# Issuing the 512-column products of one batch's MLP as two products of 256 columns

## The chip, the cores and the metric

The kernel runs on one core of a Trainium2 chip. The metric is the device time of one execution in microseconds (us), the median of several runs. TensorE multiplies, VectorE (DVE in the rows), ScalarE (ACT) and GpSimd (POOL) do the elementwise work, and the SP queue issues most transfers.

## What is computed

For every batch b (8 of them) and head h (8), the reference lets 512 tokens of width 64 read from 32 state vectors and the state vectors read from the tokens. The heads are then joined and everything goes through one MLP with a squared ReLU:

```python
scores = scale * np.matmul(x, state.transpose(0, 1, 3, 2))      # softmax over the states
xread = np.matmul(a, state)
scores2 = scale * np.matmul(state, x.transpose(0, 1, 3, 2))     # softmax over the tokens
sread = np.matmul(a2, x)
attn = np.concatenate([xread, sread], axis=2)                   # (8, 8, 544, 64)
x = attn.transpose(0, 2, 1, 3).reshape(8 * 544, 512)
h = np.maximum(x @ w_in, 0.0)                                   # w_in: 512 x 2048
return (h * h @ w_out).astype(np.float32)                       # w_out: 2048 x 512
```

## The kernel before

**Tiles and stages.** The MLP rows are worked through in nine blocks: one of 512 tokens for each batch (blocks 0 to 7), and a last one of 256 rows that holds the state reads of all batches (block 8). In blocks 0 to 7 the first layer is not applied to the token reads. Instead the state vectors are multiplied into `w_in` beforehand (tiles `w2`), so that the first layer of a block is a product of the softmax weights (tiles `k_hi`, `k_lo`) with `w2`. The hidden width of 2048 is cut into 16 chunks `fc` of 128.

**Three products for one.** To keep the precision, each operand is a pair of fp32r tiles, a high part and a low part. The helper `mm3` (its `T.matmul` is line 346) issues, for each pair of operands, high by high, high by low and low by high, all into the same PSUM tile. Every product has its own weight load.

**One chunk of a batch.** `hidden(blk, fc)` makes `ph`, a PSUM bank of 128 hidden features by 512 tokens: two contractions of 128 by three products, six products of 512 columns. ScalarE and VectorE then make the squared ReLU and split it into `g_hi` and `g_lo` (lines 898 to 906). `accumulate` takes each of the four 128-token tiles of `g` as the stationary operand and multiplies it with the chunk of `w_out` (512 columns, `wo`), again through `mm3`, into one of four PSUM accumulators `acc`: twelve products of 512 columns. So a chunk has 18 products of 512 columns, and the four accumulators of a batch are filled over all 16 chunks.

**The last block.** `hidden_reads(fc)` (lines 916 and 917) alternates products of 512 columns, where high and low parts lie side by side, with products of 256 columns, four of each in a chunk. Its second layer has two token tiles, so six products of 512 columns.

**Order.** The order of all steps is written out by hand (the strings `FIRST`, `BLOCK`, `LAST`, `READS`) and kept on each engine by `keep_order`. In batch 7 (`LAST`), `hidden.7.(n+1)` is followed by `accumulate.7.n`, with a few steps of the attention of block 8 between them. The last `accumulate.7.15` comes after `hidden.8.0`, so it lies in `READS`.

Of the kernel before, what the change touches and what calls it, by code (L numbers as in the profile page):

```python
# [239 lines left out]
def tile_attn_moe(  # L240
# [17 lines left out]
    B, H, S, D = x.shape  # L258
    Ns = state.shape[2]
    DM, DFF = w_in.shape  # L260
    P = 128
    G = 2
# [14 lines left out]
    KC = S // P  # L277
    V, A, T, SP, PL = nc.vector, nc.scalar, nc.tensor, nc.sync, nc.gpsimd
    traced, last = [0], {}
# [39 lines left out]
    def plain_w2(b, hb):  # L319
        return f"plain_w2.{b}.{hb}" in second  # L320
# [3 lines left out]
    def plain_wo(b, fc):  # L324
        return f"plain_wo.{b}.{fc}" in second
# [9 lines left out]
    def evac(key, out, src):  # L335
        if key in second:
            V.tensor_copy(out, src)  # L337
        else:
            A.copy(out, src)  # L339

    def mm3(ps, pairs, first=True, last=True):
        seq = []
        for (lh, ll), (rh, rl) in pairs:
            seq += [(lh, rh), (lh, rl), (ll, rh)]
        for i, (l, r) in enumerate(seq):
            T.matmul(ps, l, r, start=first and i == 0, stop=last and i == len(seq) - 1)  # L346
# [3 lines left out]
    def keep_busy(key, ps):  # L350

        for _ in range(BUSY.get(key, 0)):
            T.matmul(ps, ones, ones, start=True, stop=True)
# [484 lines left out]
    wo, wo_raw, wo_f = {}, {}, {}  # L838
# [30 lines left out]
    def hidden(blk, fc):  # L869
        cs = ts(fc % 2, P)  # L870
        ph = ps_h.tile([P, S], F32, tag="ph", name=f"ph{blk}_{fc}")
        keep_busy(f"hidden.{blk}.{fc}", ph[:, :P])
        if plain_w2(blk, fc // 2):
            w, k = weights[blk, fc // 2], kf[blk]
            for c in range(G):
                if c and fc < 2:
                    yield
                assert key("token_softmax", blk, c) in done
                T.matmul(ph, w[c][:, cs], k[:, c], start=c == 0, stop=c == G - 1)  # L879
        else:  # L880
            khi, klo = ks[blk]
            whi, wlo = weights[blk, fc // 2]
            mm3(ph, [((whi[:, c, cs], wlo[:, c, cs]), (khi[:, c], klo[:, c])) for c in range(khi.shape[1])])
        yield
        if plain_wo(blk, fc):
            g = p2.tile([P, S], F32, tag="g_hi", name=f"gf{blk}_{fc}", bufs=GB)
            if f"square.{blk}.{fc}" in second:
                A.activation(ph, ph, AF.Relu)
                A.activation(g, ph, AF.Square)
            else:  # L890
                r = p2.tile([P, S], F32, tag="g", name=f"r{blk}_{fc}", bufs=2)
                A.activation(r, ph, AF.Relu)
                V.scalar_tensor_tensor(g, ph, 0.0, r, ALU.max, ALU.mult)
            return g, None
        ghi = p2.tile([P, S], F32R, tag="g_hi", name=f"g_hi{blk}_{fc}", bufs=GB)
        glo = p2.tile([P, S], F32R, tag="g_lo", name=f"g_lo{blk}_{fc}", bufs=LB)
        if f"square.{blk}.{fc}" in second:
            A.activation(ph, ph, AF.Relu)  # L898
            A.activation(ph, ph, AF.Square)  # L899
        else:  # L900
            r = p2.tile([P, S], F32, tag="g", name=f"r{blk}_{fc}", bufs=2)
            A.activation(r, ph, AF.Relu)  # L902
            V.scalar_tensor_tensor(ph, ph, 0.0, r, ALU.max, ALU.mult)  # L903
        evac(f"ghi.{blk}.{fc}", ghi, ph)
        yield
        V.tensor_sub(glo, ph, ghi.bitcast(F32))  # L906
        return ghi, glo
# [19 lines left out]
        V.tensor_sub(glo, r, ghi.bitcast(F32))  # L927
        return ghi, glo

    def accumulate(acc, fc, g, tiles, first, last):  # L930
        ghi, glo = g
        for i in tiles:
            if glo is None:
                T.matmul(acc[i], ghi[:, ts(i, P)], wo[fc], start=first, stop=last)
                continue
            mm3(
                acc[i],
                [((ghi[:, ts(i, P)], glo[:, ts(i, P)]), (wo[fc][:, 0], wo[fc][:, 1]))],
                first=first,
                last=last,  # L940
            )

    out_v = out.rearrange("(b s) f -> b s f", b=B)

# [10 lines left out]
    def store(blk, acc, add):  # L955
        for i in range(KC):
            o = p2.tile([P, DM], F32, tag="o", name=f"o{blk}_{i}", bufs=OB) if add is None else add[i]
            if add is None:
                evac(f"out.{blk}.{i}", o, acc[i])
            else:  # L960
                V.tensor_add(o, acc[i], o)  # L961
            if blk < NX:
                SP.dma_start(out_v[blk, :S].rearrange("(p k) f -> k p f", k=KC)[ORDER[i]], o)
            else:
                SP.dma_start(out_v[blk, ts(i, P)], o)

    def keep_part(blk, acc):
        for i in range(KC):
            o = p2.tile([P, DM], F32, tag="o", name=f"po{blk}_{i}", bufs=OB)
            evac(f"part.{blk}.{i}", o, acc[i])  # L970
            SP.dma_start(part_d[blk][i], o)
# [10 lines left out]
    ks, weights, att, accs, gs = {}, {}, {}, {}, {}  # L982
# [8 lines left out]
    def step_hidden(blk, fc):  # L991
        if blk < B:
            ks[blk] = att[blk].k
            gs[blk, fc] = yield from hidden(blk, fc)
        else:
            gs[blk, fc] = yield from hidden_reads(fc)

    def step_reads(fc, i):
        if fc == 0 and i == 0:
            accs[B] = [ps_acc.tile([P, DM], F32, tag="acc", name=f"acc{B}_{t}") for t in range(B * Ns // P)]  # L1000
        accumulate(accs[B], fc, gs[B, fc], [i], fc == 0, fc == NFC - 1)
        yield
        if fc == NFC - 1:
            store_reads(i, accs[B][i])
# [3 lines left out]
    def step_accumulate(blk, fc):  # L1008
        sums = blk, blk < NS and fc >= PART[blk]
        of = NFC if blk >= NS else NFC - PART[blk] if sums[1] else PART[blk]  # L1010
        count[sums] = count.get(sums, 0) + 1
        first, last = count[sums] == 1, count[sums] == of
        if first:
            accs[blk] = [ps_acc.tile([P, DM], F32, tag="acc", name=f"acc{blk}_{fc}_{t}") for t in range(KC)]
        accumulate(accs[blk], fc, gs.pop((blk, fc)), range(KC), first, last)
        yield
        if last and blk < NS and not sums[1]:
            keep_part(blk, accs.pop(blk))
        elif last:
            store(blk, accs.pop(blk), parts.pop(blk, None))  # L1020

    def key(name, *index):
        return ".".join([name, *map(str, index)])
# [21 lines left out]
    for n in range(B + LATE):  # L1045
# [10 lines left out]
        if n == 0:  # L1056
            for g in range(G):
                tiles = [key("prep", n, j) for j in range(2 * g, 2 * g + 2)]
# [39 lines left out]
    for m in range(HF):  # L1098
        both = whole(f"o{m}")
        for i in range(2):  # L1100
            fc = 2 * m + i
# [16 lines left out]
    for blk in range(B + 1):  # L1118
# [14 lines left out]
        for fc in range(NFC):  # L1133
            hb = fc // 2
            if blk == B:
                needs = ["move_sread", key("split_wi", hb)]
            else:
                w = max(h for h in sets(blk) if h <= hb)
                if blk < NS and fc >= PART[blk]:
                    needs = [key("split_k", blk, g) for g in range(G)]  # L1140
                elif blk:
                    needs = [key("softmax", blk, *g) for g in groups(blk)]
                else:
                    needs = [key("token_softmax", blk, g) for g in range(1 if fc < 2 else G)]
                    needs += [key("split_kf", blk, g) for g in range(G) if hb in NP]
                needs.append(key("w2", blk, w))
            step(key("hidden", blk, fc), step_hidden, blk, fc, after=needs)
            needs = [key("hidden", blk, fc), prepared[fc] if plain_wo(blk, fc) else key("split_wo", fc // 2)]
            needs += [key("load_part", blk)] * (blk < 2 and fc == NFC - 1)
            if blk < B:  # L1150
                step(key("accumulate", blk, fc), step_accumulate, blk, fc, after=needs)
                continue
            for i in range(B * Ns // P):
                step(key("accumulate", blk, fc, i), step_reads, fc, i, after=needs)
# [50 lines left out]
```

## Time and profile before

| what | value |
|---|---|
| time before, median of 3 runs | 648.98 us (648.92 to 649.53) |
| span of the profiled execution | 647.3 us, from the first to the last instruction |
| its own time beside the span | not listed separately; the median of the runs lies 1.7 us above the span |
| TensorE products | 3738, busy 99% of the span |
| mean granted TensorE clock | 1.000 |

The span leaves out what lies before the first and behind the last instruction. A product's duration in the rows runs from its start to its last result, so neighbouring products overlap. The time that a product takes from the next one is the distance of their starts.

### The profile page before, as it was taken

To read this page: it belongs to the slowest core of one execution; us is meant where nothing else is said; L and a number is where in the kernel's file an instruction comes from. 1 tells how busy PE (TensorE), PEld (TensorE's weight loads), DVE (VectorE), ACT (ScalarE), POOL (GpSimd) and SP (SyncE) were. 2 spreads that over 40 slices of the span, in tenths; PEclk is the share of its full clock that TensorE was granted. 3 is DMA by queue.
4 is the path that set the end of the run, shared out by engine and by line. 5 is a ranking of instruction groups with operands and counts; after the bars stand their busy time and mean duration, and the time that the engine had idled before them with its cause. 6 is when DMAs were issued, how large, how long until landed. Compare 5 with 4: busy or idle time off the path is not lost.

```text
span 647.3 us, 9689 instructions
## 1 busy us (share of the span) xinstructions
PE 638.0 (99%) x3738; PEld 503.0 (78%) x3738; DVE 402.8 (62%) x660; ACT 368.8 (57%) x625; POOL 8.6 (1%) x16
## 2 busy tenths in 40 slices
PE   7999999999999999999999999999999999999997
PEld 6677777777777777777787888788878887888885
DVE  5999766665676788766855635564547444325664
ACT  6987658854756755756554535454446443544542
POOL 1200000000000000000000000000000000000000
PEclk9999999999999999999999999999999999999999
DMA  8983947250521866251254702481237321610101
GB/s 319 369 200 101 276 104 198 71 131 10 160 63 58 235 164 199 46 134 66 95 181 113 153 32 99 102 145 51 99 69 144 86 96 33 168 38 2 65 1 33
DMA packets 136590, 76.19 MB, mean 118 GB/s; under 512 B 103264, under 2 KB 121440, under 8 KB 136544
## 3 DMA queue, kind: packets, MB, share of 16 engines
q1 hardware_dynamic: 135584, 75.05, 42.5%
q8 instruction: 29, 0.48, 0.3%
q10 hardware_dynamic: 960, 0.52, 0.3%
q14 instruction: 17, 0.14, 0.1%
HBM read 50.38 MB, written 25.17 MB: 117 GB/s over the span
## 4 chain that ended last, share of the span: by engine, by line
PE 92%; DVE 3%; ACT 2%; DMA 1%; issue 0%; SPq 0%
PE acc L346 55%; PE ph L346 26%; PE w2ps L358 2%; PE ph L916 2%; PE qps L793 2%; PE ph L917 1%; PE pr L673 1%; PE sc L358 1%; DMA xn<-in_x_dram 1%; PE ph L879 1%; DMA out_dram<-o 1%; DVE o L961 0%; PE tsc L358 0%; ACT s L769 0%; PE px L472 0%
## 5 line engine op out<-in xcount | busy, mean ns | idle before, releaser
L346 PE MATMUL acc<-wo,g_hi 128*128 128x512 f32 x1088 | 336.7, 391 | 0.0
L346 PEld LDWEIGHTS acc<-wo,g_hi 128*128 128x128 f32 x1088 | 202.7, 188 | 46.4 <-issue 3.3
L346 PE MATMUL acc<-wo,g_lo 128*128 128x512 f32 x544 | 212.0, 390 | 0.4 <-DVE g_lo L906 0.4
L346 PE MATMUL ph<-k_hi,w 128*128 128x512 f32 x504 | 176.3, 394 | 0.0
L906 DVE TENSOR_TENSOR g_lo<-ph,g_hi 128x512 fp32r<-128x512 f32 x128 | 88.0, 688 | 112.4 <-ACT g_hi L339 111.6
L346 PEld LDWEIGHTS acc<-wo,g_lo 128*128 128x128 f32 x544 | 102.1, 188 | 23.2 <-DVE g_lo L906 1.0
L346 PEld LDWEIGHTS ph<-k_hi,w 128*128 128x128 f32 x504 | 94.6, 188 | 29.5 <-issue 8.0
L898 ACT ACTIVATE ph<-ph 128x512 f32<-128x512 f32 x99 | 57.8, 584 | 87.5 <-PE ph L346 86.0
L346 PE MATMUL ph<-k_lo,w 128*128 128x512 f32 x252 | 98.2, 390 | 0.0
L339 ACT CAST g_hi<-ph 128x512 fp32r<-128x512 f32 x117 | 68.7, 587 | 26.8 <-DVE ph L903 21.2
L899 ACT ACTIVATE ph<-ph 128x512 f32<-128x512 f32 x99 | 57.6, 582 | 3.1
L346 PEld LDWEIGHTS ph<-k_lo,w 128*128 128x128 f32 x252 | 47.3, 188 | 9.3
L903 DVE SCALAR_TENSOR_TENSOR ph<-ph,r 128x512 f32<-128x512 f32 x29 | 20.2, 698 | 48.9 <-ACT r L902 48.9
L902 ACT ACTIVATE r<-ph 128x512 f32<-128x512 f32 x29 | 17.3, 598 | 43.0 <-PE ph L346 43.0
L785 ACT CAST q<-wi 64x512 fp32r<-64x512 f32 x32 | 19.8, 619 | 15.0 <-PE qps L793 12.6
L797 DVE COPY qo<-qps 128x512 f32<-128x512 f32 x32 | 20.6, 683 | 9.7 <-PE qps L793 7.1
L754 DVE TENSOR_TENSOR w<-w2ps,w 128x512 fp32r<-128x512 f32 (+1 forms) x34 | 20.1, 634 | 8.0 <-ACT w L339 8.0
L339 ACT CAST w<-w2ps 128x512 fp32r<-128x512 f32 (+1 forms) x26 | 13.6, 567 | 20.2 <-DVE w L337 11.5
L788 DVE TENSOR_TENSOR q<-wi,q 64x512 fp32r<-64x512 f32 x32 | 22.0, 686 | 1.9 <-ACT q L785 1.0
L916 PE MATMUL ph<-sr,s 128*128 128x512 f32 x64 | 23.1, 396 | 0.0
L358 PE MATMUL w2ps<-wi,stT 64*32 64x512 f32 (+1 forms) x288 | 18.5, 554 | 1.4 <-DVE wi L369 0.7
L815 DVE TENSOR_TENSOR w<-w2r,w 128x1024 fp32r<-128x1024 f32 x16 | 19.5, 1219 | 0.6 <-ACT w L812 0.3
(127 smaller groups left out, 525.4 us busy)
## 6 DMA issues: line engine op xcount, KB each, us to landing
out_dram<-o SPq DMA_DIRECT2D x33, 256.0 KB, 2.6
w_d<-qo SPq DMA_DIRECT2D x32, 256.0 KB, 2.4
w2r<-w_d SPq DMA_DIRECT2D x16, 512.0 KB, 4.7
wo_raw<-in_moe_w_out_dram SPq DMA_DIRECT2D x16, 511.8 KB, 7.7
wi_raw<-in_moe_w_in_dram SPq DMA_DIRECT2D x16, 511.5 KB, 6.2
xp<-in_x_dram SPq DMA_DIRECT2D x112, 64.0 KB, 2.5
e_d<-eB SPq DMA_DIRECT2D x32, 128.0 KB, 3.3
eT<-e_d SPq DMA_DIRECT2D x8, 512.0 KB, 4.0
```

The lines of the kernel that those rows point to most:

```text
L339: A.copy(out, src)
L346: T.matmul(ps, l, r, start=first and i == 0, stop=last and i == len(seq) - 1)
L358: T.matmul(ps, l, r, start=True, stop=True)
L754: V.tensor_sub(w[:, u, g, 1], ps[g], w[:, u, g, 0].bitcast(F32))
L785: A.copy(t[u, g], wi[h][u, j])
L788: V.tensor_sub(t[v, g], wi[h][u, j], t[u, g].bitcast(F32))
L797: V.tensor_copy(os[g], ps[:, g])
L898: A.activation(ph, ph, AF.Relu)
L899: A.activation(ph, ph, AF.Square)
L903: V.scalar_tensor_tensor(ph, ph, 0.0, r, ALU.max, ALU.mult)
L906: V.tensor_sub(glo, ph, ghi.bitcast(F32))
L916: T.matmul(ph.rearrange("p i n -> p (i n)"), whi[:, c, cs], both, start=c == 0, stop=False)
```

## The change

For the last whole batch (block 7, `blk == B - 1`) the first layer is issued in two halves of 256 tokens, each with its own six products. The second layer is issued, for each token tile, in two halves of 256 output columns, each with its own three products. The start flag is given only in the first half. The stationary operands are the same in both halves, and each half loads them again. Blocks 0 to 6 and the last block are as before.

```diff
@@ hidden(blk, fc)
+        elif blk == B - 1:
+            khi, klo = ks[blk]
+            whi, wlo = weights[blk, fc // 2]
+            for u in range(2):
+                t = ts(u, S // 2)
+                mm3(ph[:, t], [((whi[:, c, cs], wlo[:, c, cs]), (khi[:, c, t], klo[:, c, t])) for c in range(G)], u == 0, u == 1)
         else:
@@ accumulate
-    def accumulate(acc, fc, g, tiles, first, last):
+    def accumulate(acc, fc, g, tiles, first, last, halves=1):
...
-            mm3(
-                acc[i],
-                [((ghi[:, ts(i, P)], glo[:, ts(i, P)]), (wo[fc][:, 0], wo[fc][:, 1]))],
-                first=first,
-                last=last,
-            )
+            for u in range(halves):
+                c = ts(u, DM // halves)
+                mm3(
+                    acc[i][:, c],
+                    [((ghi[:, ts(i, P)], glo[:, ts(i, P)]), (wo[fc][:, 0, c], wo[fc][:, 1, c]))],
+                    first=first and u == 0,
+                    last=last and u == halves - 1,
+                )
@@ step_accumulate
-        accumulate(accs[blk], fc, gs.pop((blk, fc)), range(KC), first, last)
+        accumulate(accs[blk], fc, gs.pop((blk, fc)), range(KC), first, last, 2 if blk == B - 1 else 1)
```

## Rows read from the trace of the kernel before

**Rows 1.** Page, part 1: busy time, share of the span and instructions of each engine.

```profile
span 647.3 us, 9689 instructions
...
PE 638.0 (99%) x3738; PEld 503.0 (78%) x3738; DVE 402.8 (62%) x660; ACT 368.8 (57%) x625; POOL 8.6 (1%) x16
```

**Rows 2.** Page, part 4: the chain that ended last, by engine.

```profile
PE 92%; DVE 3%; ACT 2%; DMA 1%; issue 0%; SPq 0%
```

**Rows 3.** Chain in order of time, in batch 7: start us, us, what.

```profile
557.45 1.36 PE ph L346 x6
558.81 2.72 PE acc L346 x12
561.53 1.36 PE ph L346 x6
```

**Rows 4.** Waits from 520 to 595.3 us: total, times, longest.

```profile
DVE g_lo L906 <- ACT g_hi L339: 26.0, 14, 3.4
ACT ph L898 <- PE ph L346: 15.7, 9, 2.3
...
ACT r L902 <- PE ph L346: 11.3, 7, 2.2
```

**Rows 5.** Line 346, 526.4 to 599.4 us: count, duration ns min/median/max, starts, forms.

```profile
L346 PE MATMUL acc<-wo,g_hi x136: 389/389/396, 527.8 to 599.0; 128*128 128x512 f32 x136
...
L346 PE MATMUL ph<-k_hi,w x64: 389/389/500, 526.5 to 592.3; 128*128 128x512 f32 x64
L346 PEld LDWEIGHTS ph<-k_lo,w x32: 187/188/189, 526.5 to 591.9; 128*128 128x128 f32 x32
```

**Rows 6.** Windows: busy us (count) per engine, granted clock, DMA share, GB/s.

```profile
526.40:595.20 68.80, 68.80 (x433) 55.94 (x433) 28.76 (x46) 33.26 (x56) 0.00 (x0) 1.00 0.29 79
595.20:637.10 41.90, 41.90 (x213) 34.90 (x213) 28.43 (x54) 19.29 (x39) 0.00 (x0) 1.00 0.07 26
```

**Rows 7.** Timeline of the state reads' first layer: 12 pairs, 632.91 to 637.14.

```profile
632.91 0.39 PE L916 MATMUL ph<-sr,s 128*128 128x512 f32 x1
...
633.14 0.28 PE L917 MATMUL ph<-sr,s 128*128 128x256 f32 x1
633.14 0.19 PEld L916 LDWEIGHTS ph<-sr,s 128*128 128x128 f32 x1
633.25 0.40 PE L916 MATMUL ph<-sr,s 128*128 128x512 f32 x1
...
633.48 0.28 PE L917 MATMUL ph<-sr,s 128*128 128x256 f32 x1
...
633.60 0.40 PE L916 MATMUL ph<-sr,s 128*128 128x512 f32 x1
...
637.14 0.62 PE L346 MATMUL acc<-wo,g_hi 128*128 128x512 f32 x2
```

**Rows 8.** Line 917, whole span: count, duration ns min/median/max.

```profile
L917 PE MATMUL ph<-sr,s x64: 274/281/284, 595.5 to 637.0; 128*128 128x256 f32 x64
```

**Rows 9.** Timeline: streams of 128-column fp32 products, each with a weight load.

```profile
15.20 0.53 PEld L353 LDWEIGHTS ph<-const-float32-1.0 128*128 128x128 f32 x4
15.31 0.61 PE L353 MATMUL ph<-const-float32-1.0 128*128 128x128 f32 x4
...
36.19 1.03 PE L472 MATMUL px<-ident,xn 128*128 128x128 f32 x8
```

**Rows 10.** Durations of those products: by-form busy us and mean ns; line 472 min/median/max.

```profile
L353 PE MATMUL ph<-const-float32-1.0 128*128 128x128 f32 x4 | 0.6, 274 | 0.0
...
L472 PE MATMUL px<-ident,xn x16: 270/272/273, 31.2 to 37.0; 128*128 128x128 f32 x16
```

**Rows 11.** Timeline around `accumulate.7.15`.

```profile
596.25 0.69 DVE L906 TENSOR_TENSOR g_lo<-ph,g_hi 128x512 fp32r<-128x512 f32 x1 [0.65 <-ACT g_hi L339]
...
596.66 0.63 PE L346 MATMUL acc<-wo,g_hi 128*128 128x512 f32 x2
596.99 0.19 PEld L346 LDWEIGHTS acc<-wo,g_lo 128*128 128x128 f32 x1
...
597.12 0.39 PE L346 MATMUL acc<-wo,g_lo 128*128 128x512 f32 x1
```

**Rows 12.** Timeline: a run of 64 short products in batch 7.

```profile
569.62 1.10 PE L673 MATMUL pr<-xn,eT 128*32 128x64 f32 x64
```

## Prediction

> **What bounds the kernel now.** I read the page's busy shares first. TensorE is busy for 99% of the span, VectorE for 62%, ScalarE for 57% [rows 1]. A busy share alone can mislead, since products overlap, so the chain of work that ended last comes next: 92% of it is TensorE [rows 2]. In batch 7, where the change is made, the chain is nothing but products: six of the first layer in 1.36 us, twelve of the second in 2.72 us, six again [rows 3]. The reader should see that these add up without a gap, 4.08 us for the 18 products of a chunk, which is 226.7 ns for each, whichever layer it is. The waits say the same from the other side: what ScalarE waits for in this stretch is TensorE, 15.7 us and 11.3 us in the two forms of the squared ReLU, and VectorE waits behind ScalarE [rows 4]. So a nanosecond that a product of batch 7 gains or loses goes into the end of the kernel at full size, and the other engines can't pay for it or take it up. The granted clock is 1.00 both in batch 7 and in the state reads behind it, which is the 2.4 GHz level [rows 6].
>
> **What the change removes and adds.** In the stretch of batch 7 the rows count 136 second-layer products with `g_hi`, thus 68 with `g_lo`, of which twelve belong to `accumulate.6.15`; that leaves 192, and the first layer has 64 and 32, so 96 [rows 5]. These 288 products of 512 columns go, and 576 of 256 columns come, each with its own weight load. TensorE's count rises from 3738 to 4026. Nothing is moved: no transfer, no queue and no semaphore wait of another engine is touched, ScalarE still waits for the last product into `ph`, and the store still waits for the last into `acc`. The columns streamed are the same. All of the cost is therefore the price of cutting one product in two: twice the distance between starts of 256-column products, less 226.7 ns.
>
> **The price of a 256-column product.** No stretch of this trace runs 256-column fp32r products one behind the other, so the price has to be bounded.
>
> From the product of 512: at 2.4 GHz 512 columns need 213.3 ns, and the distance is 226.7 ns, so 13.4 ns come on top. If they are a fixed price of each product with its weight load, 256 columns cost 106.7 + 13.4 = 120 ns, and a split costs 240 - 226.7 = 13.4 ns. If they grow with the columns, 256 cost 113.3 ns and a split costs nothing.
>
> From the nearest row: the first layer of the state reads alternates 512 and 256 columns with the same kinds of operands. Twelve such pairs go from 632.91 to 637.14 us, 4.23 us, or 352.5 ns for a pair [rows 7]. Start to start, a 256-column product takes 0.11 to 0.12 us and the 512-column one 0.23 us. So the pair is 12.5 ns longer than 340 ns, which it would be if price went by columns alone, and that reading is contradicted in this stretch at least. With 13.4 ns each it would be 346.7 ns, which is nearest, though 6 ns short. If instead the 512-column product costs its usual 226.7 ns here too, the 256-column one costs 125.8 ns, and a split 24.9 ns.
>
> From below: the other streams of short products with a weight load for each have 128 columns of plain fp32. The four at 15.31 us take 0.61 us, less one duration of 0.274 us, over three distances: 112 ns. The eight at 36.19 us give (1.03 - 0.272) / 7 = 108 ns [rows 9, 10]. The former hold the array as long as 256 columns of fp32r do, since their duration, 274 ns, is the shortest of the 256-column ones [rows 8, 10]. They show that a product with a load each can come every 112 ns, over short runs and with other operands.
>
> The ends are thus 108 and 125.8 ns, and I take 120: it is what the fixed price gives, and it is close to the distances of 0.11 to 0.12 us read directly in rows 7. The sum: 288 x 13.4 ns = 3.86 us. By chunk, 4.08 us become 4.32 us.
>
> By the Trainium skill's page "TensorE: Matmul & The Clock Gate", section "Back-to-back issue gap", a product follows the one before after its columns at 2.4 GHz plus about 2.5 ns, 215.8 ns for 512 columns. The trace does not agree, it has 226.7 ns; by that rule a split would cost 2.5 ns and the change 0.7 us.
>
> **One wait.** The second half of each tile's products comes later than before, but the first one with `g_lo` comes sooner: it is the third product of a tile, now two short products behind the first instead of two long ones, 0.24 us in place of 0.46. Everywhere in batch 7 but at its end a whole `hidden` lies between, 1.36 us or more, and covers this. In `accumulate.7.15` it is near: VectorE writes `g_lo` from 596.25 to 596.94, the load of it starts at 596.99 and its product at 597.12 [rows 11]. With the first product at the same distance from `g_lo` the load would start 0.2 us too early and wait for at most that; but `accumulate.7.14`, which lies between, is 12 x 13.4 ns = 0.16 us longer, so 0.05 us are left. Behind it on TensorE is only the rest of that accumulation. The bounds are 0 and 0.2 us.
>
> **Sum.** 3.86 + 0.05 = 3.9 us on the span of 647.3 us, so 651.2 us. The runs' median of 648.98 lies 1.7 us above the span, and the change touches nothing outside it: 648.98 + 3.9 = 652.9 us.
>
> **The rivals.**
>
> *The weight load becomes the bound.* A 256-column product leaves only some 110 ns for the next load, whose duration is 0.19 us and which starts as the product does [rows 7]. If that load sets the pace, every 256-column product costs the 125.8 ns that the pair leaves it: 24.9 ns x 288 = 7.2 us, 656.2 us. For it: the pair is longer than the fixed price explains. Against it: the four products of rows 9 have loads that take as long (0.53 us for four, which overlap) and come every 112 ns. The same page of the Trainium skill, section "LDWEIGHTS (loading the stationary operand)", gives a load as its columns over 1.2 GHz, 107 ns for 128, as long as the 256 columns themselves stream; that speaks for this rival, and the trace shows neither load alone.
>
> *The price goes by columns.* Then 113.3 ns for each half, no change, 649.0 us. For it: in rows 7 the first 256-column product takes 0.11 us. Against it: the pair's 352.5 ns. A stream of nothing but 256-column products could still settle at this pace.
>
> *It ends faster.* If what stretches 512 columns from 213.3 to 226.7 ns belongs to long streams, and halves go at the pace of the eight products in rows 9, 108 ns, a split saves 226.7 - 216 = 10.7 ns and the change 3.1 us: 645.9 us. It decides from 111 ns down, where 288 splits save 1.3 us. Against it: not one of the distances in rows 7 is below 0.11 us.
>
> *Something dearer.* If products or loads queued for issue, or a product had to wait for the whole of its load, a half would cost up to 0.19 us: 2 x 188 - 226.7 = 149 ns, 43 us in all, 692 us. Rows 7 speak against it, since there a product starts 0.11 us behind its load of 0.19 us, and so does the run of 64 short products with 64 loads in 1.10 us [rows 12], against which two instructions every 120 ns are few.
>
> **How the numbers follow.** Forecast (117 to 122 ns for a half, 651 to 654 us): 0.46. Weight load: 0.24. Price by columns: 0.18. Faster: 0.05. Dearer: 0.07. The range runs from the pace by columns, with 0.4 us for the scatter of the runs, to the weight load's price with as much and the 0.2 us of the wait: 648.6 to 656.8 us. It leaves out the last two cases and the edges of the others. A change of 0.2%, 1.3 us, is about what a measurement can tell from none. So faster 0.05, same 0.18, slower 0.77.
>
> **What would show it.** In the chain of the kernel after, a chunk of batch 7 should read about 1.44 us for twelve products and 2.88 us for 24. The distance between starts of the halves is the whole question: 0.120 us by my sum, 0.126 by the weight load's, 0.113 by columns. Line 346 should show 576 products of 128x256, with the shortest durations near 274 ns. The state reads should start 3.9 us later and be no longer than now, the granted clock should stay at 1.00, and only `accumulate.7.15` may show a wait for `g_lo`. A fallen clock, or waits of TensorE within batch 7, would make the prediction wrong for another reason than the price.

## The result, and the profile after

The changed kernel takes 652.88 us, the median of four runs (652.68 to 654.15), beside 649.25 us for the kernel before (648.92 to 649.85, a fourth run beside the three of the table). The ratio is 1.0064, with a 95% interval of 1.0051 to 1.0078. In microseconds that is 3.3 to 5.1 us more, and 3.6 us between the medians. The forecast was 3.9 us more, 652.9 us.

The profiled execution of the changed kernel is its slowest run, 654.15 us. These are the lines of its page that answer to [rows 1, 2]:

```profile
span 652.4 us, 10262 instructions
...
PE 643.5 (99%) x4026; PEld 520.4 (80%) x4026; DVE 402.5 (62%) x660; ACT 368.9 (57%) x625; POOL 8.6 (1%) x16
...
PE 93%; DVE 3%; ACT 2%; DMA 1%; issue 0%; SPq 0%
```

TensorE has the 4026 products of the forecast, and the chain is still made of them. The span is 5.1 us longer, more than the medians differ by, and the first thing to settle is where the rest lies. It lies at the start, far from the change. A transposed tile of batch 0 starts at 8.78 us before:

```profile
8.78 0.33 PE L472 MATMUL px<-ident,xn 128*128 128x128 f32 x1
```

and at 10.07 us in the profile after:

```profile
10.07 0.33 PE L472 MATMUL px<-ident,xn 128*128 128x128 f32 x1
```

The delay comes before anything that the change touches, and 1.26 us of it are left where batch 7 begins (526.61 us in the chain before, 527.87 after). It is also by as much (1.27 us) that this run lies above the median. What remains, 5.1 - 1.3 = 3.8 us, is the change.

In batch 7 the chain in order of time reads so (start us, us, what), as the counterpart of [rows 3]:

```profile
560.19 1.44 PE ph L346 x12
561.63 2.88 PE acc L346 x24
564.51 1.44 PE ph L346 x12
...
573.15 1.03 PE pr L673 x64
574.18 1.63 PE ph L346 x12
```

Twelve halves take 1.44 us and 24 take 2.88 us, 120.0 ns each, and a chunk has grown from 4.08 to 4.32 us. The timeline shows the single steps, and how the loads go with them:

```profile
564.35 0.28 PE L346 MATMUL ph<-k_hi,w 128*128 128x256 f32 x1
564.35 0.19 PEld L346 LDWEIGHTS ph<-k_lo,w 128*128 128x128 f32 x1
564.47 0.28 PE L346 MATMUL ph<-k_lo,w 128*128 128x256 f32 x1
```

The load for the product at 564.47 starts at 564.35, with the product before its own, and its duration of 0.19 us runs on beyond that product's step of 0.12. By line, over batch 7, and by window, the counterparts of [rows 5, 6] are:

```profile
L346 PE MATMUL acc<-wo,g_hi x262: 280/283/397, 529.1 to 603.8; 128*128 128x256 f32 x127, 128*128 128x512 f32 x4
```

```profile
526.40:600.20 73.80, 73.80 (x716) 71.79 (x715) 30.35 (x47) 33.96 (x58) 0.00 (x0) 1.00 0.27 74
600.20:642.20 42.00, 42.00 (x226) 35.63 (x226) 28.07 (x54) 19.24 (x39) 0.00 (x0) 1.00 0.07 26
```

In the first line the forms are counted on every second product. The granted clock (third number from the end) is 1.00, as before. The busy time of the weight loads (the second pair) is 97% of the window of batch 7, where it was 81% [rows 6]. From the first product of the state reads to the last of the kernel it is 47.26 us (600.13 to 647.39) beside 47.11 (595.26 to 642.37); `accumulate.7.15`, which lies there, explains the difference: twelve splits at 13.3 ns are 0.16 us. In that same `accumulate.7.15` TensorE does not wait for `g_lo` (counterpart of [rows 11]):

```profile
600.67 0.69 DVE L912 TENSOR_TENSOR g_lo<-ph,g_hi 128x512 fp32r<-128x512 f32 x1 [0.65 <-ACT g_hi L339]
...
601.54 0.40 PE L346 MATMUL acc<-wo,g_hi 128*128 128x256 f32 x2
601.78 0.29 PE L346 MATMUL acc<-wo,g_lo 128*128 128x256 f32 x1
```

`g_lo` is written by 601.36, before the first product starts.

### The profile page after: what moved, and what is told of

Read it like the earlier page. It is cut to its first block, busy times and chain, and to the rows that moved or that the text cites. A ratio compares the mean times of both kernels' runs of the same rounds, so it can differ in the third digit from the quotient of the medians.

```text
span 652.4 us, 10262 instructions
## 1 busy us (share of the span) xinstructions
PE 643.5 (99%) x4026; PEld 520.4 (80%) x4026; DVE 402.5 (62%) x660; ACT 368.9 (57%) x625; POOL 8.6 (1%) x16
## 4 chain that ended last, share of the span: by engine, by line
PE 93%; DVE 3%; ACT 2%; DMA 1%; issue 0%; SPq 0%
PE acc L346 55%; PE ph L346 26%; PE w2ps L358 2%; PE ph L922 2%; PE qps L793 2%; PE ph L923 1%; PE pr L673 1%; PE sc L358 1%; PE px L472 1%; DMA out_dram<-o 1%; PE ph L879 1%; DMA std<-in_state_dram 1%; PE tsc L358 0%; DVE o L969 0%; ACT s L769 0%
## 5 line engine op out<-in xcount | busy, mean ns | idle before, releaser
L346 PE MATMUL acc<-wo,g_hi 128*128 128x512 f32 (+1 forms) x1216 | 344.0, 368 | 0.0
L346 PEld LDWEIGHTS acc<-wo,g_hi 128*128 128x128 f32 x1216 | 218.6, 189 | 41.4 <-issue 3.3
L346 PE MATMUL acc<-wo,g_lo 128*128 128x512 f32 (+1 forms) x608 | 223.3, 367 | 0.4 <-DVE g_lo L912 0.4
L346 PE MATMUL ph<-k_hi,w 128*128 128x512 f32 (+1 forms) x568 | 179.6, 369 | 0.0
L346 PEld LDWEIGHTS acc<-wo,g_lo 128*128 128x128 f32 x608 | 114.7, 189 | 20.5 <-DVE g_lo L912 1.0
L346 PEld LDWEIGHTS ph<-k_hi,w 128*128 128x128 f32 x568 | 103.6, 189 | 27.1 <-issue 8.0
L346 PE MATMUL ph<-k_lo,w 128*128 128x512 f32 (+1 forms) x284 | 103.8, 366 | 0.0
L346 PEld LDWEIGHTS ph<-k_lo,w 128*128 128x128 f32 x284 | 53.6, 189 | 8.2
```

## The experiments

All times are medians, and each is set beside runs of the kernel before on the same chip (648.7 to 649.05 us).

**One layer at a time.** First the first layer alone in halves:

```diff
-        accumulate(accs[blk], fc, gs.pop((blk, fc)), range(KC), first, last, 2 if blk == B - 1 else 1)
+        accumulate(accs[blk], fc, gs.pop((blk, fc)), range(KC), first, last)
```

> Only the first layer of batch 7 is issued in halves (96 products become 192), the second layer as before. Fixed price of 13.3 ns for each product with its weight load: 96 x 13.3 ns = 1.3 us over the kernel before, about 650.4 us, and halves start 0.120 us apart. Rival, the cost comes from the second layer alone (its moving operand, its accumulators): no change here, 649.1 us.

Measured: 650.34 us, ratio 1.0021 (1.0012 to 1.0030), 1.3 us more. Then the second layer alone:

```diff
-        elif blk == B - 1:
+        elif False:
             khi, klo = ks[blk]
```

> Only the second layer of batch 7 is issued in halves (192 products become 384), the first layer as before. Fixed price: 192 x 13.3 ns = 2.6 us over the kernel before, about 651.7 us, twice the cost of the first layer alone. Rival, the cost is not a price of the single product but something that the change causes once in the stretch (a wait, the clock): this run and the one with the first layer alone don't add up to the whole change.

Measured: 651.98 us, ratio 1.0045 (1.0032 to 1.0057), 2.9 us more. Both layers pay, the second about twice as much, as it has twice the products. So the cost is one of single products and not of the second layer alone or of one place. The two add up to 4.2 us, within the interval of the whole change. The chains show why they could come out a little above it. With the first layer alone a chunk reads:

```profile
557.81 1.43 PE ph L346 x12
559.24 2.75 PE acc L346 x12
```

and with the second alone:

```profile
559.14 1.39 PE ph L346 x6
560.52 2.87 PE acc L346 x24
```

The layer that is left whole takes 0.03 us more than in [rows 3] (2.75 for 2.72, 1.39 for 1.36). Products of 512 columns that come behind shorter ones are a little slower at first.

**Five batches.** The same change in batches 3 to 7:

```diff
-        elif blk == B - 1:
+        elif blk >= 3:
...
-        accumulate(accs[blk], fc, gs.pop((blk, fc)), range(KC), first, last, 2 if blk == B - 1 else 1)
+        accumulate(accs[blk], fc, gs.pop((blk, fc)), range(KC), first, last, 2 if blk >= 3 else 1)
```

> Both layers in halves in batches 3 to 7: 5 x 288 = 1440 products are cut. Fixed price: 1440 x 13.3 ns = 19.2 us over the kernel before, about 668.3 us. If earlier batches hide a part behind other work (waits of TensorE that a slower stream takes up), less; if the denser issue or the shorter time for weight loads builds up a delay over a long stream, more, up to 1440 x 24.9 ns = 36 us.

Measured: 666.98 us, ratio 1.0281 (1.0265 to 1.0296), 17.9 us more (17.2 to 19.2). With five times the products it is 12.5 ns a split; 1440 splits at the fixed price make 19.2 us, which the interval only just holds. No delay builds up: a chunk in batch 4 or later still reads 1.44 and 2.88 us:

```profile
349.96 1.44 PE ph L346 x12
351.40 2.88 PE acc L346 x24
```

The traces confirm that something is missing: from a product ahead of all splits (239.99 us before, 239.41 with five batches cut) to the last one (642.37 and 659.75) it is 18.0 us more, so 1.2 us less than 19.2. Almost half of it lies in one place, where TensorE waited before. The kernel before has

```profile
322.06 0.39 PE L346 MATMUL acc<-wo,g_lo 128*128 128x512 f32 x1
322.49 1.45 PE L793 MATMUL qps<-q,s 128*128 128x512 f32 x4
323.78 0.39 PE L346 MATMUL ph<-k_hi,w 128*128 128x512 f32 x1
```

and with five batches cut it reads

```profile
324.93 0.28 PE L346 MATMUL acc<-wo,g_lo 128*128 128x256 f32 x1
325.05 1.09 PE L793 MATMUL qps<-q,s 128*128 128x512 f32 x4
325.97 0.28 PE L346 MATMUL ph<-k_hi,w 128*128 128x256 f32 x1
```

The four products of `qps`, whose loads waited for VectorE's `q` before, take 0.92 us in place of 1.29, and the last product with `g_lo` takes 0.24 us (two halves of 0.12) in place of 0.43. That is 0.56 us. A wait of TensorE for `g_lo` in batch 3 got shorter by about 0.2 (0.4 before, 0.2 after). The rest, some 0.5 us, is spread in small pieces. It fits what batch 7 shows behind its run of 64 short products: the first layer there takes 1.58 us before (from 570.72 us) and 1.63 after (574.18), 0.05 us for six splits in place of 0.08, since the whole products were slower there than 226.7 ns already.

**The same weights twice in a row.** The halves alternate, so that each stationary operand is loaded at least twice in succession (a high part four times, since it stands in two of the three products) and neighbouring products write different halves of the bank. A helper does it for both layers of batch 7:

```diff
+    CUTS = ((0, 256), (256, 512))
+    def mm3x(ps, pairs, first=True, last=True):
...
+        seq = [(l, r, a, b) for l, r in seq for a, b in CUTS]
+        for i, (l, r, a, b) in enumerate(seq):
+            T.matmul(ps[:, a:b], l, r[:, a:b], start=first and i == 0, stop=last and i == len(seq) - 1)
```

> As the change, but the halves alternate: each stationary operand is loaded twice in a row, and neighbouring products write different halves of the bank. Fixed price of product and load: the same as the change, 652.9 us, halves 0.120 us apart. Rival, the 13.3 ns come from adding to the same columns of PSUM right behind the product before: halves 0.107 to 0.110 us apart, 288 x 10 ns = 3 us faster than before, 646 us. Rival, a load of weights that are there already is cheaper: also faster than the change.

Measured: 652.52 us, ratio 1.0052 (1.0040 to 1.0065), and the chain has the same steps (line 356 is the matmul of the new helper):

```profile
562.62 1.44 PE ph L356 x12
564.06 2.88 PE acc L356 x24
```

Both rivals fall. At 256 columns it makes no difference whether the columns of PSUM were written by the product right before, nor whether the weights are those that the array just had.

**Uneven cuts.** The forecast's price was columns at 2.4 GHz plus 13.3 ns (13.4 in its own rounding). It gives the same sum for every cut in two, so cuts of other sizes test it. The same kernel with other `CUTS`:

```diff
-    CUTS = ((0, 256), (256, 512))
+    CUTS = ((0, 320), (320, 512))
```

> Each product of batch 7 is cut into 320 and 192 columns, alternating. Fixed price: 133.3 + 80 + 2 x 13.3 = 240 ns, the same as two halves, so 652.9 us. Rival, the weight load of 128 columns sets the pace of a short product, at 120 ns: 146.7 + 120 = 266.7 ns, 288 x 40 ns = 11.5 us over the kernel before, 660.5 us; at the 112 ns of the short streams at the start of the trace: 258.7 ns, 9.2 us, 658.2 us.

Measured: 657.85 us, ratio 1.0134 (1.0118 to 1.0149), 9.0 us more. And with 384 and 128 columns:

```diff
-    CUTS = ((0, 256), (256, 512))
+    CUTS = ((0, 384), (384, 512))
```

> Each product of batch 7 is cut into 384 and 128 columns, alternating. Fixed price: 173.3 + 66.7 = 240 ns, again 652.9 us. Rival, the weight load sets the pace of the short one, at 112 to 120 ns: 285 to 293 ns, 288 x 59 to 67 ns = 17 to 19 us over the kernel before, 666 to 668 us.

Measured: 666.6 us, ratio 1.0266 (1.0252 to 1.0280), 17.7 us more. Here the fixed price alone is wrong, and both times come near what the rival gives, a weight load that sets the pace of the short part at the 112 ns of [rows 9, 10]: 658.2 and 666 us. The chains, of the first cut:

```profile
560.33 1.54 PE ph L356 x12
561.87 3.08 PE acc L356 x24
```

and of the second:

```profile
564.69 1.72 PE ph L356 x12
566.41 3.44 PE acc L356 x24
```

Pairs take 257 ns (1.54 / 6 and 3.08 / 12) and 287 ns (1.72 / 6 and 3.44 / 12). Take from each what the long part costs by the fixed price, 146.7 and 173.3 ns, and 110 and 113 ns are left for the short part, where its columns and the fixed price would make 93.3 and 66.7. The timeline of the second cut shows how this is read:

```profile
569.35 0.30 PEld L356 LDWEIGHTS acc<-wo,g_lo 128*128 128x128 f32 x2
569.40 0.45 PE L356 MATMUL acc<-wo,g_lo 128*128 128x384 f32 x2
569.63 0.30 PEld L356 LDWEIGHTS ph<-k_hi,w 128*128 128x128 f32 x2
569.69 0.45 PE L356 MATMUL ph<-k_hi,w 128*128 128x384 f32 x2
```

Two loads, each of 0.19 us, are over in 0.30 us, so they follow each other by 0.11 us; then a step of the long product has to pass before the next two (569.35 to 569.63 is 0.28 us, less 0.11). By the starts alone the pair is divided otherwise: a long product starts 0.06 us behind the short one (569.63, where the load starts with it, to 569.69), and the next short one 0.23 us behind the long one (569.40 to 569.63). So the wait for a load shows in the long product, and 110 and 113 ns are shares of the pair's sum, not distances.

**Cuts in three.** With no part long enough to cover a load, the load's pace stands by itself:

```diff
-    CUTS = ((0, 256), (256, 512))
+    CUTS = ((0, 172), (172, 344), (344, 512))
```

> Each product of batch 7 is cut into 172, 172 and 168 columns, so that no product is long enough to cover a weight load. If a product's distance is its columns at 2.4 GHz plus 13.3 ns, whatever its length: 253.3 ns for the three, 288 x 26.7 ns = 7.7 us over the kernel before, 656.6 us. If it is that or about 112 ns, whichever is more, as the two uneven cuts suggest: 336 ns, 288 x 109 ns = 31.5 us over the kernel before, 680.4 us, with products and loads both 0.11 us apart.

Measured: 680.07 us, ratio 1.0482 (1.0452 to 1.0512), 31.4 us more. Chain:

```profile
563.92 2.00 PE ph L356 x18
565.92 4.02 PE acc L356 x36
```

4.02 us for 36 products is 111.7 ns each in the mean, where the fixed price makes 84.4. The loads show the same pace:

```profile
565.68 0.75 PEld L356 LDWEIGHTS acc<-wo,g_hi 128*128 128x128 f32 x6
```

Six loads, each of 0.19 us, are over in 0.75 us, 0.11 us from one to the next. It is not a least distance of products as such: in [rows 12] 64 products, whose loads have 32 columns, take 1.10 us, and in the uneven cut products start 0.06 us apart. The Trainium skill, "TensorE: Matmul & The Clock Gate", section "LDWEIGHTS (loading the stationary operand)", gives a load as its columns over 1.2 GHz, by estimate 107 ns for 128 columns. The trace is near it, 5 ns above.

**The state reads' pair.** [Rows 7] gave 352.5 ns for a pair of 512 and 256 columns, 6 ns over the fixed price. Two kernels, made from the kernel before, ask what these belong to. The first groups the products by length:

```diff
         for c in range(NC):
             both = k[:, c].rearrange("p i n -> p (i n)")
             T.matmul(ph.rearrange("p i n -> p (i n)"), whi[:, c, cs], both, start=c == 0, stop=False)
+        for c in range(NC):
             T.matmul(ph[:, 0], wlo[:, c, cs], k[:, c, 0], start=False, stop=c == NC - 1)
```

> The kernel before, with the first layer of the state reads in another order: in each chunk first the four products of 512 columns, then the four of 256, in place of alternating pairs. By the fixed price a pair should take 226.7 + 120 = 346.7 ns, and it took 352.5. If the 6 ns are a price of going from 256 to 512 columns, three of four such steps go in each chunk: 16 x 3 x 6 ns = 0.3 us faster than before, 648.8 us, seen in the trace rather than in the time. If they belong to the 256-column product: no change.

Measured: 648.95 beside 648.86 us, ratio 0.9995 (0.9986 to 1.0004), no difference that the times can tell. In its chain a chunk's first layer takes 0.91 + 0.47 = 1.38 us, against 1.40 to 1.41 before (350 to 352.5 ns a pair):

```profile
602.40 0.91 PE ph L916 x4
603.31 0.47 PE ph L918 x4
603.78 1.39 PE acc L346 x6
```

The second layer behind it still takes 1.39 us where six products at 226.7 ns make 1.36. The second kernel cuts the 512-column products of this layer in halves:

```diff
-            both = k[:, c].rearrange("p i n -> p (i n)")
-            T.matmul(ph.rearrange("p i n -> p (i n)"), whi[:, c, cs], both, start=c == 0, stop=False)
+            for i in range(2):
+                T.matmul(ph[:, i], whi[:, c, cs], k[:, c, i], start=c == 0 and i == 0, stop=False)
```

> The kernel before, with each 512-column product of the state reads' first layer issued as two of 256, so that this layer has 256-column products alone: twelve in a chunk. Fixed price: 12 x 120 = 1440 ns for a chunk, against 4 x 352.5 = 1410 ns, 16 x 30 ns = 0.5 us over the kernel before. Rival, each 256-column product costs 125.8 ns: 1510 ns, 1.6 us over the kernel before.

Measured: 649.74 us, ratio 1.0010 (1.0000 to 1.0019), 0 to 1.2 us more, which holds the 0.5 of the fixed price and not the 1.6 of the rival. In its timeline the twelve products of a chunk go from 602.42 to 603.86 us, 120 ns each:

```profile
602.42 0.40 PE L916 MATMUL ph<-sr,s 128*128 128x256 f32 x2
...
603.86 0.63 PE L346 MATMUL acc<-wo,g_hi 128*128 128x512 f32 x2
```

So a 256-column product behind its like costs 120 ns in this layer too, and the 6 ns belong to the alternation.

## Why the prediction was right, point by point

**The bound.** TensorE's stream sets the end in batch 7, and what its products lose comes out at full size: 0.24 us in a chunk, 16 chunks, 3.84 us, beside 3.8 us in the span once the start is taken off and 3.6 us in the medians. That the time itself, 652.88 us, meets the forecast of 652.9 is in part luck: the difference came out 0.3 us smaller, and the median before is 0.3 us above the one that it was added to. The five batches show the limit of the bound: where TensorE waited for others, some 0.7 of 19.2 us were taken up.

**The price.** The term that carried the forecast was 120 ns for half a product, taken from bounds of 108 and 125.8 ns, and it measured 120.0 ns. The uneven cuts and the thirds show that it was right for a narrower reason than I gave. What a product adds to the stream is the larger of two times: the columns at 2.4 GHz plus 13.3 ns, or some 112 ns, the pace of weight loads. That gives 258.7, 285.3 and 336 ns for the three cuts, which measured 257, 287 and 335. At 256 columns the first is 120 ns and wins by 8 ns. By this rule parts below (112 - 13.3) x 2.4 = 237 columns cost more than the fixed price says; that is an estimate, as no run has a length between 192 and 256. The prediction's other rule, 2.5 ns for each product, stands in the Trainium skill, "TensorE: Matmul & The Clock Gate", section "Back-to-back issue gap", as the gap of a product taken by itself; the prediction left out this condition, and in this stream, where each product has a load, it is 13.3 ns.

**The rival of the weight load** named the right mechanism and gave it the wrong size. 125.8 ns came from charging all that the pair had too much to the 256-column product, which costs 120 ns among its like in that layer too. The load's own pace is 112 ns, which stood in [rows 9, 10] and was used only as a bound from below.

**The rivals by columns and faster** fall with the 120 ns, in either order of the halves. The dearer one falls too: over 1440 splits a chunk still takes 1.44 and 2.88 us.

**The wait for `g_lo`** did not come. The forecast allowed 0.05 us and bounds of 0 and 0.2. In the profile after, `g_lo` is begun 0.87 us before the first product of `accumulate.7.15`, where it was 0.41 us before; the longer `accumulate.7.14` explains 0.16 us of that. The prediction took `g_lo` to follow `hidden.7.15`, but VectorE is held up by other work, first in the kernel before, then after:

```profile
592.76 2.22 DVE L333 TENSOR_TENSOR sr<-srn,sr 128x1024 fp32r<-128x1024 f32 x1 [1.37 <-ACT sr L339]
597.22 2.21 DVE L333 TENSOR_TENSOR sr<-srn,sr 128x1024 fp32r<-128x1024 f32 x1 [1.36 <-ACT sr L339]
```

The next step of chunk 15 on VectorE starts as this ends, at 594.91 and 599.30 us, though its operand `r` from ScalarE is ready by 593.40 and 598.11. `sr` comes from ScalarE, which begins it behind its work on chunk 14 (590.57 and 595.04 us), so the longer `accumulate.7.13` and `hidden.7.15` add to the lead as well, 0.16 and 0.08 us, and of the 0.46 us all but 0.06 is explained.

**What stays open.** Each product of these kernels has its own weight load, so the runs do not tell whether the 13.3 ns are paid by the product or by the exchange of weights.

## What to carry to other kernels

Where TensorE is the chain, a product costs more than its columns: here 13.3 ns for each product with its load, 6% at 512 columns and 12.5% at 256, so cutting a product in halves without need costs 13.3 ns each time. Look for the second limit as well, the pace at which weights can be loaded, 112 ns here for 128 columns, since a product below some 237 columns, by estimate, no longer covers it. Bound a price by the nearest rows, but ask of each such row which of the limits it shows.

## What was not expected

Products of 512 columns are a little slower for a while behind shorter ones. Behind a run of 256-column products a whole layer takes 0.03 us more, six or twelve products alike, and a pair of alternating lengths takes 352.5 ns where the single steps make 346.7. Grouping the lengths gives 0.02 us back in a chunk, too little for the times to show. What causes it was not found.
